# Order of the last filter inputs, the first queries and the keys' remainder in the head of a fused attention and spectral filter kernel

## The chip, the cores and the metric

The kernel runs on one core of a Trainium2 chip. What counts is the device time of one execution in microseconds, as the median over several executions. Two kernels that differ in the order of their work in the first 70 us are compared.

## What is computed

Two independent branches over S = 2048 positions and D = 448 channels are concatenated along the last axis:

```python
# A: attention, 16 query heads of 28 channels share one key and one value head
q = (x @ wq).reshape(B, S, 16, 28).transpose(0, 2, 1, 3)
k, v = x @ wk, x @ wv
p = softmax(einsum("bhqd,bkd->bhqk", q, k) * 28 ** -0.5)
a = einsum("bhqk,bkd->bhqd", p, v).transpose(0, 2, 1, 3).reshape(B, S, 448) @ wo
# B: a filter in the frequency domain
X = rfft2(x, axes=(-2, -1)) * (w_r + 1j * w_i)
b = irfft2(X, s=(S, D), axes=(-2, -1))
return concatenate([a, b], axis=-1)
```

All inputs are fp32. Products that need fp32 accuracy are made of two or three products of a rounded high part and a remainder (tiles ending in `h` and `l`).

## The kernel before

The kernel has a **head** (to about 68 us) and an **attention phase**. The attention phase runs 256 steps, each one group of four heads, one column of 512 queries and one block of 128 keys: four score matmuls (L917, 128x512, weights `ka`, moving `qa`), four exponentials on ACT (L852, or L928 and L942 for the scores set aside in tiles `k`), and four products with the values `vs` (L863). The later stages of the filter and the output projection are spread over these steps by a list (`PLAN`), and PE, ACT and DVE follow the order of the program.

The head does four things side by side:

- **Projection.** Twelve numbered groups (`group(n)`, preceded by a first column) multiply input and weights on PE (L369), and ACT evicts each result to `qraw` (L373); DVE takes each row's largest magnitude (L374), which `terms` turns into `prod` (L296) and `shift` into a bound `cvec` (a small matmul L301 and a DVE copy L302).
- **Keys.** `fetch` gathers half of the keys into `kf`. `keys(h)` for that half makes the high part on ACT (L287), the remainder `kl` on DVE (L288), and sends three copies (L293, on the sync queue) into `ka`: one of the high part, two of the remainder. Each half fills 64 columns of each of the 16 key blocks, so every score matmul reads both halves.
- **First queries.** `build_q(0, 0, True)` computes `ql` on DVE (L232), its high part `qh` on ACT (L229) and the remainder back into `ql` on DVE (L218). Sixteen copies (`copy_q(i, p, ...)`, head i, part p) then put them into `qa`: part 0 by DVE (L205), part 1 by ACT (L203), part 2 by the sync queue and part 3 by the GpSimd (POOL) queue (both L206).
- **Filter, first stages.** Eight inputs q = 0 to 7 of 512 KB (`xb`, L120) with a filter each (`fw`, L124). `fft1_fold(q)` is six DVE instructions (L129 to L134); `fft1_a(q)` 64 matmuls (L155) and two evictions on ACT into tiles `a` (L144); `fft1_b(q)` 16 matmuls (L172) into two PSUM tiles, evicted to `bs` by ACT for q < 6 (L180) and by DVE for q = 6, 7 (L182), and two stores of 225 KB to DRAM on the sync queue (L185). In a pair `fft1_b(q, q + 1)` the first takes two banks of their own, and the second takes two of the rotating banks.

PSUM has six rotating banks: `bank()` hands them out in turn. At the end of the head they are unpacked as `d, f, a, b, e, c = free` and put into the order in which attention takes them first. `a` was the bank of the last shift, `d` and `f` those of the last `fft1_a`, `b` that of the largest bound (`pb3`, read by L504), and `e` and `c` the two of `fft1_b(7)`.

PE's order is that of the program throughout, ACT's and DVE's from `group(4)` on (L451). The issue order on the sync and GpSimd queues is chosen when the program is built, after the order in the program and the time at which an instruction is thought to be ready. The attention phase starts when the last matmul of the head (L503) has been issued; `vs` comes from a transpose on DVE (L505) at the end of DVE's part of the head.

Of the kernel before, what the change touches and what calls it, by code (L numbers as in the profile page):

```python
# [10 lines left out]
F32 = mybir.dt.float32  # L11
# [4 lines left out]
ALU = mybir.AluOpType  # L16
# [6 lines left out]
DF = D // 2 + 1  # L23
# [49 lines left out]
def kernel(ctx: ExitStack, tc: tile.TileContext, t: dict):  # L73
    nc = tc.nc
# [4 lines left out]
    fp = ctx.enter_context(tc.tile_pool(name="fp", bufs=2))  # L79
# [8 lines left out]
    ka = cp.tile([128, S], F32R, name="ka")  # L88
# [4 lines left out]
    t1 = dp.tile([64, 64, DF], F32, name="t1")  # L93
# [10 lines left out]
    def aux2(name):  # L104
        return aux_pool[0].tile([128, 2, DF], F32, name=name, tag="aux")
# [9 lines left out]
    def fft1_load(q, parts=(0, 1)):  # L115
        if q > 7:
            return
        if 0 in parts:
            x = fp.tile([128, 4, 256], F32, name="xb", tag=("wr", "b2")[q % 2])
            nc.sync.dma_start(x, t["xb"][q])  # L120
            xb[q] = [x, None]
        if 1 in parts:
            w = xb[q][1] = fp.tile([128, 4, 64], F32, name="fw", tag=("ph", "pl")[q % 2])
            nc.sync.dma_start(w, t["fw"][:, 4 * q:4 * q + 4])  # L124

    def fft1_fold(q):
        x = xb[q][0][:113]
        f = fp.tile([113, 4, 256], F32, name="f", tag="wi")
        nc.vector.tensor_tensor(f[:, 0:2], x[:, 0::2], x[:, 1::2], op=ALU.add)  # L129
        nc.vector.tensor_tensor(f[:, 2:4], x[:, 0::2], x[:, 1::2], op=ALU.subtract)  # L130
        nc.vector.tensor_tensor(x[:, 0], f[:, 0], f[:, 1], op=ALU.add)
        nc.vector.tensor_tensor(x[:, 1], f[:, 0], f[:, 1], op=ALU.subtract)
        nc.vector.tensor_tensor(x[:, 2], f[:, 2], f[:, 3], op=ALU.subtract)
        nc.vector.tensor_tensor(x[:, 3], f[:, 2], f[:, 3], op=ALU.add)  # L134
        ff[q] = x.rearrange("p k (j h m) -> p k j h m", h=2, m=32)

    at1, stored = {}, []

    def fft1_a(*qs):
        for q in qs:  # L140
            for p in range(2):
                pa = fft1_a_mm(q, p)
                a = at1[q, p] = fp.tile([128, 2, DF], F32, name="a", tag=("pwr", "pwi")[p])
                nc.scalar.activation(a, pa, AF.Copy)  # L144
            fft1_load(q + 4, (0,))
# [10 lines left out]
                           start=True, stop=True)  # L156
        return pa

    def fft1_b(*qs):
        for i, q in enumerate(qs):  # L160
            fft1_out(q, fft1_mm(q, [pair_of(bank()) for _ in range(2)] if i else None))
            fft1_load(q + 4, (1,))

    def fft1_mm(q, pb=None):
        w = xb[q][1]
        if pb is None:
            pb = aux2("pbb"), ps_o.tile([128, 2, DF], F32, name="po")
        for p in range(2):
            a = at1.pop((q, p))
            for h in range(2):  # L170
                for e in range(2):
                    mm(pb[h][64 * e:64 * e + 64, p], w[64 * h:64 * h + 64, 2 * p + e], a[64 * h:64 * h + 64, e],  # L172
                       start=True, stop=True)
        return pb

    def fft1_out(q, pb):
        bs = fp.tile([128, 2, 2, DF], F32, name="bs", tag="cst" if q < 6 else "b2")
        for h in range(2):
            if q < 6:
                nc.scalar.activation(bs[:, h], pb[h], AF.Copy)  # L180
            else:
                nc.vector.tensor_copy(bs[:, h], pb[h])  # L182
        for e in range(2):
            n0 = 16 * e + 2 * q
            stored.append(nc.sync.dma_start(t1.rearrange("s (l n) f -> s l n f", l=2)[:, :, n0:n0 + 2],  # L185
                                            bs[64 * e:64 * e + 64]))

    def fft2_consts():
        for n in ("g1", "g2"):
# [9 lines left out]
    def copy_q(i, p, q, src, eng):  # L199

        o, x = q[32 * p:32 * p + 32, i], src[32 * i:32 * i + 32].bitcast(F32)
        if eng is nc.scalar:
            return eng.activation(o, x, AF.Copy)  # L203
        if eng is nc.vector:
            return eng.tensor_copy(o, x)  # L205
        return eng.dma_start(o.bitcast(F32), x)  # L206

    def build_q(c, g, first=False):
        cs = slice(c * CW, (c + 1) * CW)
        qh = qp.tile([128, CW], F32R, name="qh", bufs=1)  # L210
        ql = qp.tile([128, CW], F32R, name="ql", bufs=1)
        qt = ql.bitcast(F32)
        if (c, g) not in qa:
            qa[c, g] = qp.tile([128, 4, CW], F32R, name="qa")
        q = qa[c, g]

        def split():
            nc.vector.tensor_tensor(ql, qt, qh.bitcast(F32), op=ALU.subtract)  # L218
            if first:
                return  # L220
            for i in range(4):
                for p, src in enumerate((qh, ql)):
                    mv = nc.sync.dma_start(q[32 * p:32 * p + 32, i].bitcast(F32), src[32 * i:32 * i + 32].bitcast(F32))
                    behind(mv, b2["last", 0] if (c, g) == (0, 1) else stored[-1])
            nc.sync.dma_start(q[64:128].bitcast(F32), q[0:64].bitcast(F32))

        def high():
            if first:
                return nc.scalar.activation(qh, qt, AF.Copy)  # L229
            return nc.vector.tensor_copy(qh, qt)  # L230

        ops = [(540, lambda: nc.vector.tensor_scalar(qt, qraw[:, g, cs], mask, cvec[:, g, c:c + 1],  # L232
                                                     op0=ALU.mult, op1=ALU.add)),
               (450, high), (710, split)]
        if not first:
            return ops
        for _, op in ops:
            op()
        return q, qh, ql
# [9 lines left out]
    def bank():  # L249
        free.rotate(-1)  # L250
        return free[-1]

    def pair_of(b):
        return b[:, :2 * DF].rearrange("p (n f) -> p n f", n=2)


    with tc.tile_pool(name="w1", bufs=1) as w1:
# [24 lines left out]
        def keys(h):  # L282
            hs = slice(h * 1024, h * 1024 + 1024)
            kl = w1.tile([32, 1024], F32R, name="kl")
            src = kf[:, hs].rearrange("p (s t j) -> p s t j", s=2, j=32)
            high = ka[:32].rearrange("p (t s j) -> p s t j", s=NC, j=32)[:, 2 * h:2 * h + 2]
            nc.scalar.activation(high, src, AF.Copy)  # L287
            nc.vector.tensor_tensor(kl.rearrange("p (t s j) -> p s t j", s=2, j=32), src, high.bitcast(F32),  # L288
                                    op=ALU.subtract)
            kt = ka.rearrange("p (t x) -> p t x", t=16)[:, :, 64 * h:64 * h + 64]  # L290
            low = kl.rearrange("p (t x) -> p t x", t=16)
            for p, src in ((1, kt[:32]), (2, low), (3, low)):
                nc.sync.dma_start(kt[32 * p:32 * p + 32].bitcast(F32), src.bitcast(F32))  # L293

        def terms(c0, c1):
            return nc.vector.tensor_scalar(prod[:, :, c0:c1], qmx[:, :, c0:c1], kmb, None, op0=ALU.mult)  # L296
# [1 line left out]
        def shift(c0, c1):  # L298
            b = bank()[:, :NG * (c1 - c0)]
            pb = b.rearrange("p (g c) -> p g c", g=NG)  # L300
            mm(b, blk, prod[:, :, c0:c1], start=True, stop=True)  # L301
            nc.vector.tensor_copy(cvec[:, :, c0:c1], pb)  # L302

        halves = slice(0, 1024), slice(1024, 2048)
        with tc.tile_pool(name="x1", bufs=2) as x1:
# [125 lines left out]
            def group(n):  # L431
                c, g = 1 + n // 4, n % 4
                pq = pq1[g] if c == 1 else bank()
                for j in range(1 if c == 1 else 0, NK):
                    proj(pq, *xs[c], g, j)
                if n == 10:
                    key_max()
                evac(c, g, pq)
# [18 lines left out]
            for j in range(NK):  # L457
                split_x(*xs[3], 3, j)
            group(5)
            keys(0)  # L460
            group(6)
            fft1_fold(4)
            group(7)
            for v in range(3):
                fetch_v(range(7, 14), v)
            fft1_b(0, 1)
            fft1_a(2, 3)
            fft1_fold(5)
            group(8)
            group(9)  # L470
# [4 lines left out]
            terms(0, 1)  # L475
            fft1_fold(7)
            fetch_v(range(7, 12), 3)
            fft1_b(2, 3)
            keys(1)
            fft1_a(4, 5)  # L480
            shift(0, 1)
            qf, qh, ql = build_q(0, 0, True)
            group(11)
            terms(1, NC)


        for i in range(4):
            copy_q(i, 2, qf, qh, nc.sync)
            copy_q(i, 0, qf, qh, nc.vector)
            copy_q(i, 3, qf, ql, nc.gpsimd)  # L490
        fetch_v(range(12, 14), 3)
        copy_q(0, 1, qf, ql, nc.scalar)
        fft1_b(4, 5)
        copy_q(1, 1, qf, ql, nc.scalar)
        fft1_a(6, 7)
        for i in (2, 3):
            copy_q(i, 1, qf, ql, nc.scalar)
        shift(1, NC)
        nc.vector.tensor_reduce(cmax, cvec, axis=AX.X, op=ALU.max)
        pb3 = bank()  # L500
        fft1_b(6, 7)
        for g in range(NG):
            mm(pb3[0:1, 4 * g:4 * g + 4], cmax[:, g:g + 1], sel4, start=True, stop=True)  # L503
        nc.vector.tensor_reduce(bits, pb3[0:1, 0:16], axis=AX.X, op=ALU.max)  # L504
# [4 lines left out]

    d, f, a, b, e, c = free  # L510
    free.clear()
    free.extend((a, d, f, e, c, b))
    spare = a, b, d
    free = [[0.0, bank] for bank in free]
    clock = {"pe": 0.0, "act": 0.0, "dve": 0.0}
# [65 lines left out]
    b2 = {}  # L581
# [602 lines left out]
```

## Time and profile before

| | |
|---|---|
| three runs, us | 632.76, 632.44, 632.50 |
| median, us | 632.5 |
| profiled execution, us | 633.24 |
| its span (first to last instruction), us | 631.5 |
| granted TensorE clock, mean | 1.00 |

The rows of the profile that follow in the prediction have these columns. In a timeline: start in us from the span's beginning, duration, engine, line, operation, what is written and read, shape, number of merged instructions, and in brackets the idle time of the engine before it with what ended that. PEld is the loading of matmul weights, which overlaps the matmuls; SPq is an issue on the sync queue. Consecutive matmuls overlap, so a matmul's length says little, and the distance from start to start is its cost. In a table of windows: the stretch and its length, then for PE, PEld, DVE, ACT and POOL the busy time (number of instructions), then the clock, the mean busy share of the DMA engines and the GB/s moved. In a list of DMA issues the last number is the median time from issue to landing.

### The profile page before, as it was taken

The numbers are of one execution on the slowest core, as the hardware profiler recorded it, in microseconds if no ns is written. First come the engines' busy times: TensorE is split into PE (matmuls) and PEld (weight loads), VectorE is DVE, ScalarE is ACT, GpSimd is POOL, SyncE is SP. The second block draws the span as 40 slices with busy tenths as digits, with TensorE's granted clock in tenths as the row PEclk, the third lists the DMA queues.
The fourth block names the chain that finished last, engine by engine and source line by source line (L and its number), as shares of the span: only waits on it lengthen the run. The fifth ranks groups of instructions, "written<-read, shape, count | busy, mean of one in ns | idle before, by whom it ended". The sixth has DMA issues, their size and how long they took to land. (4 is left out here: it accounts for less than half of the span.)

```text
span 631.5 us, 12130 instructions
## 1 busy us (share of the span) xinstructions
PE 625.5 (99%) x4420; PEld 377.6 (60%) x4420; DVE 430.2 (68%) x775; ACT 547.2 (87%) x986; POOL 67.4 (11%) x132
## 2 busy tenths in 40 slices
PE   9999999999999999999999999999999999999997
PEld 7888545655555556646555665555556565555555
DVE  5996458779999944857766845277687764457753
ACT  5565999999999998988899989999989989989991
POOL 3522211011203110000110100001010100000000
PEclk9999999999999999999999999999999999999999
DMA  8857773446456523126340513034152413030001
GB/s 255 290 162 199 215 181 99 103 132 184 121 156 144 149 56 83 59 70 184 80 113 6 128 35 82 16 84 147 42 122 60 111 46 89 16 82 15 17 30 62
DMA packets 40931, 66.71 MB, mean 106 GB/s; under 512 B 11189, under 2 KB 25926, under 8 KB 39904
## 3 DMA queue, kind: packets, MB, share of 16 engines
q1 hardware_dynamic: 35232, 52.50, 30.4%
q0 software_dynamic: 5056, 12.45, 7.6%
q8 instruction: 36, 0.59, 0.4%
q10 hardware_dynamic: 576, 0.92, 0.4%
q14 instruction: 31, 0.25, 0.1%
HBM read 29.77 MB, written 17.87 MB: 75 GB/s over the span
## 5 line engine op out<-in xcount | busy, mean ns | idle before, releaser
L852 ACT ACTIVATE p<-s 128x512 f32<-128x512 f32 x392 | 217.8, 646 | 24.9 <-PE s L917 23.9
L917 PE MATMUL s<-qa,ka 128*128 128x512 f32 x736 | 222.6, 402 | 0.0
L917 PEld LDWEIGHTS s<-qa,ka 128*128 128x128 f32 x736 | 134.5, 188 | 58.6 <-issue 26.2
L863 PE MATMUL s<-p,vs 128*32 128x512 f32 x1144 | 141.7, 595 | 0.0
L923 DVE COPY k<-s 128x512 f32<-128x512 f32 x119 | 78.2, 685 | 68.1 <-PE s L917 67.9
L942 ACT ACTIVATE k<-k 128x1024 f32<-128x1024 f32 x80 | 83.4, 1140 | 0.0
L852 ACT ACTIVATE qraw<-s 128x512 f32<-128x512 f32 x136 | 78.0, 646 | 2.3 <-PE s L917 2.3
L863 PEld LDWEIGHTS s<-p,vs 128*32 128x32 f32 x1144 | 34.3, 109 | 76.2 <-issue 69.7
L852 ACT ACTIVATE p<-po 128x512 f32<-128x512 f32 x88 | 57.2, 650 | 6.5 <-PE po L917 6.4
L917 PE MATMUL po<-qa,ka 128*128 128x512 f32 x151 | 60.9, 404 | 0.0
L917 PE MATMUL sx<-qa,ka 128*128 128x512 f32 x137 | 55.2, 403 | 0.0
L863 PE MATMUL s<-qraw,vs 128*32 128x512 f32 x424 | 54.8, 593 | 0.0
L863 PE MATMUL s<-k,vs 128*32 128x512 f32 x352 | 46.3, 594 | 0.0
L852 ACT ACTIVATE p<-sx 128x512 f32<-128x512 f32 x64 | 42.0, 656 | 3.0 <-PE sx L917 2.9
L738 POOL DMA_DIRECT2D ol<-ol x36 | 18.0, 508 | 229.3 <-DVE ol L761 157.2
L867 DVE STREAM_TRANSPOSE osb<-s 128x512 f32<-128x512 f32 x15 | 10.7, 716 | 38.9 <-PE s L863 38.8
L917 PEld LDWEIGHTS po<-qa,ka 128*128 128x128 f32 x151 | 28.4, 188 | 13.6 <-issue 6.7
L917 PEld LDWEIGHTS sx<-qa,ka 128*128 128x128 f32 x137 | 25.7, 188 | 11.0 <-issue 4.2
L863 PEld LDWEIGHTS s<-qraw,vs 128*32 128x32 f32 x424 | 13.2, 110 | 29.9 <-issue 28.7
L863 PEld LDWEIGHTS s<-k,vs 128*32 128x32 f32 x352 | 11.0, 110 | 25.1 <-issue 24.2
L852 ACT ACTIVATE qraw<-sx 128x512 f32<-128x512 f32 x35 | 22.7, 648 | 2.0 <-PE sx L917 2.0
L923 DVE COPY p<-s 128x512 f32<-128x512 f32 x37 | 24.1, 682 | 0.0
(260 smaller groups left out, 926.2 us busy)
## 6 DMA issues: line engine op xcount, KB each, us to landing
qa<-qa SPq DMA_DIRECT2D x15, 512.0 KB
raw<-xa SPq DMA_DIRECT2D x16, 256.0 KB
xb<-xb SPq DMA_DIRECT2D x8, 512.0 KB
qa<-qh SPq DMA_DIRECT2D x64, 64.0 KB
qa<-ql SPq DMA_DIRECT2D x60, 64.0 KB
t<-bs SPq DMA_DIRECT2D x16, 225.0 KB
wr<-wr POOLq DMA_DIRECT2D x16, 225.0 KB, 3.9
wi<-wi POOLq DMA_DIRECT2D x16, 225.0 KB, 5.1
```

What stands on the lines that cost most here:

```text
L738: nc.gpsimd.dma_start(ol[c][o, g].bitcast(F32), ol[c][r, 0].bitcast(F32))
L852: nc.scalar.activation(tiles[-1][:, h % 2], sc, AF.Exp, scale=SCALE)
L863: mm(po[c, g][32 * i:32 * i + 32], vs[:, kc], ps[i // 2][:, i % 2], start=(n == 1), stop=(n == 16))
L867: nc.vector.transpose(o, po[c, g])
L917: begun.append(mm(sc, ka[:, kc * 128:(kc + 1) * 128], qa[c, g][:, h], start=True, stop=True))
L923: nc.vector.tensor_copy(keep[i][h // 2][:, h % 2], sc)
L942: nc.scalar.activation(p, p, AF.Exp, scale=SCALE)
```

## The change

Stores are taken out of `fft1_b` into a function `fft1_store(q)`, which also loads the filter q + 4. `fft1_b` handles one q; its second argument says whether it takes rotating banks. `keys` returns a function `finish` with the remainder and the three sends. The order in the head becomes: the loads of inputs 6 and 7 (issued by `fft1_a(2, 3)`) ahead of the stores of q = 1; the high part of the second half of the keys behind `fft1_a(4, 5)`; then shift and first queries, all sends of the queries, two DVE copies and one ACT copy; then the keys' remainder and its sends; then group 11. One copy (head 3, part 1) goes from ACT to DVE, one (head 2, part 1) from behind to ahead of the evictions of `fft1_a(6, 7)`, and the second eviction of `fft1_b(7)` from DVE to ACT. The order of the banks changes in its last three places. Nothing is added to or left out of the computation.

```diff
-    def fft1_b(*qs):
-        for i, q in enumerate(qs):
-            fft1_out(q, fft1_mm(q, [pair_of(bank()) for _ in range(2)] if i else None))
-            fft1_load(q + 4, (1,))
...
+    def fft1_b(q, other=False):
         w = xb[q][1]
+        pb = [pair_of(bank()) for _ in range(2)] if other else (aux2("pbb"), ps_o.tile([128, 2, DF], F32, name="po"))
...
+        bs = stored[q] = fp.tile([128, 2, 2, DF], F32, name="bs", tag="cst" if q < 6 else "b2")
         for h in range(2):
-            if q < 6:
+            if q < 6 or q + h == 8:
                 nc.scalar.activation(bs[:, h], pb[h], AF.Copy)
             else:
                 nc.vector.tensor_copy(bs[:, h], pb[h])
+
+    def fft1_store(q):
         for e in range(2):
             n0 = 16 * e + 2 * q
...
+            stored[-1] = nc.sync.dma_start(t1.rearrange("s (l n) f -> s l n f", l=2)[:, :, n0:n0 + 2],
+                                           stored[q][64 * e:64 * e + 64])
+        fft1_load(q + 4, (1,))
...
             nc.scalar.activation(high, src, AF.Copy)
...
+            def finish():
+                nc.vector.tensor_tensor(kl.rearrange("p (t s j) -> p s t j", s=2, j=32), src, high.bitcast(F32),
+                                        op=ALU.subtract)
...
+                for p, x in ((1, kt[:32]), (2, low), (3, low)):
+                    nc.sync.dma_start(kt[32 * p:32 * p + 32].bitcast(F32), x.bitcast(F32))
+            return finish
...
-            keys(0)
+            keys(0)()
...
-            fft1_b(0, 1)
+            fft1_b(0)
+            fft1_store(0)
+            fft1_b(1, True)
             fft1_a(2, 3)
+            fft1_store(1)
...
-            fft1_b(2, 3)
-            keys(1)
+            fft1_b(2)
+            fft1_store(2)
+            fft1_b(3, True)
+            fft1_store(3)
             fft1_a(4, 5)
+            finish_keys = keys(1)
             shift(0, 1)
             qf, qh, ql = build_q(0, 0, True)
+            for i in range(4):
+                copy_q(i, 2, qf, qh, nc.sync)
+                copy_q(i, 3, qf, ql, nc.gpsimd)
+            for i in (0, 1):
+                copy_q(i, 0, qf, qh, nc.vector)
+            copy_q(0, 1, qf, ql, nc.scalar)
+            finish_keys()
             group(11)
             terms(1, NC)
...
-        for i in range(4):
-            copy_q(i, 2, qf, qh, nc.sync)
+        for i in (2, 3):
             copy_q(i, 0, qf, qh, nc.vector)
-            copy_q(i, 3, qf, ql, nc.gpsimd)
         fetch_v(range(12, 14), 3)
-        copy_q(0, 1, qf, ql, nc.scalar)
-        fft1_b(4, 5)
         copy_q(1, 1, qf, ql, nc.scalar)
+        fft1_b(4)
+        fft1_store(4)
+        fft1_b(5, True)
+        fft1_store(5)
+        copy_q(2, 1, qf, ql, nc.scalar)
         fft1_a(6, 7)
-        for i in (2, 3):
-            copy_q(i, 1, qf, ql, nc.scalar)
+        copy_q(3, 1, qf, ql, nc.vector)
         shift(1, NC)
...
-        fft1_b(6, 7)
+        fft1_b(6)
+        fft1_store(6)
+        fft1_b(7, True)
+        fft1_store(7)
...
-    free.extend((a, d, f, e, c, b))
+    free.extend((a, d, f, c, b, e))
```

More of the change, by code (lines that the diff above doesn't have):

```diff
@@ L135, in fft1_fold @@
         ff[q] = x.rearrange("p k (j h m) -> p k j h m", h=2, m=32)
-    at1, stored = {}, []
+    at1, stored = {}, {}
     def fft1_a(*qs):
@@ L157, in fft1_a_mm @@
         return pa
-    def fft1_b(*qs):
-        for i, q in enumerate(qs):
-            fft1_out(q, fft1_mm(q, [pair_of(bank()) for _ in range(2)] if i else None))
-            fft1_load(q + 4, (1,))
-    def fft1_mm(q, pb=None):
+    def fft1_b(q, other=False):
         w = xb[q][1]
-        if pb is None:
-            pb = aux2("pbb"), ps_o.tile([128, 2, DF], F32, name="po")
+        pb = [pair_of(bank()) for _ in range(2)] if other else (aux2("pbb"), ps_o.tile([128, 2, DF], F32, name="po"))
         for p in range(2):
@@ L173, in fft1_mm @@
                        start=True, stop=True)
-        return pb
-    def fft1_out(q, pb):
-        bs = fp.tile([128, 2, 2, DF], F32, name="bs", tag="cst" if q < 6 else "b2")
+        bs = stored[q] = fp.tile([128, 2, 2, DF], F32, name="bs", tag="cst" if q < 6 else "b2")
         for h in range(2):
-            if q < 6:
+            if q < 6 or q + h == 8:
                 nc.scalar.activation(bs[:, h], pb[h], AF.Copy)
@@ L182, in fft1_out @@
                 nc.vector.tensor_copy(bs[:, h], pb[h])
+    def fft1_store(q):
         for e in range(2):
             n0 = 16 * e + 2 * q
-            stored.append(nc.sync.dma_start(t1.rearrange("s (l n) f -> s l n f", l=2)[:, :, n0:n0 + 2],
-                                            bs[64 * e:64 * e + 64]))
+            stored[-1] = nc.sync.dma_start(t1.rearrange("s (l n) f -> s l n f", l=2)[:, :, n0:n0 + 2],
+                                           stored[q][64 * e:64 * e + 64])
+        fft1_load(q + 4, (1,))
     def fft2_consts():
@@ L287, in keys @@
             nc.scalar.activation(high, src, AF.Copy)
[L288 to L293, printed above, removed]
+            def finish():
+                nc.vector.tensor_tensor(kl.rearrange("p (t s j) -> p s t j", s=2, j=32), src, high.bitcast(F32),
+                                        op=ALU.subtract)
+                kt = ka.rearrange("p (t x) -> p t x", t=16)[:, :, 64 * h:64 * h + 64]
+                low = kl.rearrange("p (t x) -> p t x", t=16)
+                for p, x in ((1, kt[:32]), (2, low), (3, low)):
+                    nc.sync.dma_start(kt[32 * p:32 * p + 32].bitcast(F32), x.bitcast(F32))
+            return finish
         def terms(c0, c1):
```

## The prediction

> **What bounds the kernel now.** I read the page first, then stretches of 10 us and of 1 us, then the timeline of each engine around the one stretch that was not full.
>
> ```profile
> span 631.5 us, 12130 instructions
> ...
> PE 625.5 (99%) x4420; PEld 377.6 (60%) x4420; DVE 430.2 (68%) x775; ACT 547.2 (87%) x986; POOL 67.4 (11%) x132
> ```
> ```profile
> 50.00:60.00 10.00, 10.00 (x187) 8.37 (x185) 7.95 (x18) 5.44 (x11) 2.48 (x5) 1.00 0.65 202
> ...
> 80.00:90.00 10.00, 9.91 (x51) 5.66 (x53) 3.95 (x7) 10.00 (x23) 1.92 (x4) 1.00 0.78 175
> ```
> ```profile
> 65.00:66.00 1.00, 0.50 (x10) 0.30 (x2) 0.34 (x2) 0.98 (x3) 1.00 (x2) 1.00 0.82 246
> ```
>
> The columns behind the stretch are its length and the busy time of PE, PEld, DVE, ACT and POOL, then clock, DMA share and GB/s. PE is the bound, at clock 1.00. The change touches only the head, and from 20 us on the head has one hole, at 65 to 72 us, where it hands over to attention. From 80 to 90 us, in early attention, ACT is as full as PE, so attention runs only as soon as both have started: what moves the first exponential moves everything behind it, up to the end. PE from the second hand-over of filter work to the third group of scores, weight loads where they say who was late:
>
> ```profile
> 60.19 0.41 PE L172 MATMUL pbb<-a,fw 64*64 64x225 f32 x2
> ...
> 61.87 3.30 PE L155 MATMUL s<-cs,xb 113*32 113x113 f32 x128
> 65.11 0.39 PE L301 MATMUL s<-prod,blk 128*128 128x12 f32 x2
> 66.04 0.41 PE L172 MATMUL pbb<-a,fw 64*64 64x225 f32 x2 [0.54 <-ACT a L144]
> ...
> 67.89 0.34 PE L503 MATMUL s<-sel,cmax 128*1 128x4 f32 x8
> 68.17 2.44 PE L917 MATMUL s<-qa,ka 128*128 128x512 f32 x8
> ...
> 71.85 0.50 PE L917 MATMUL s<-qa,ka 128*128 128x512 f32 x1
> ...
> 73.89 1.06 PE L863 MATMUL s<-k,vs 128*32 128x512 f32 x8
> 74.78 1.07 PE L863 MATMUL s<-p,vs 128*32 128x512 f32 x8
> 75.77 0.50 PE L917 MATMUL sx<-qa,ka 128*128 128x512 f32 x1
> ```
> ```profile
> 69.40 0.76 PEld L917 LDWEIGHTS s<-qa,ka 128*128 128x128 f32 x4 [0.33 <-DVE bs L182]
> ```
> ```profile
> 70.88 0.14 PEld L863 LDWEIGHTS s<-k,vs 128*32 128x32 f32 x2 [0.19 <-ACT k L928]
> ```
>
> From 65.11 to 71.85 PE takes 6.74 us for work that elsewhere takes 0.39 (shift) + 1.68 (a pair of second filter stages, 61.87 - 60.19) + 0.28 (68.17 - 67.89) + 2.04 (eight scores, 73.89 - 71.85) + 0.99 (one key block times values, 75.77 - 74.78) = 5.38. The hole is 1.36 us: 0.71 ahead of the first score, where PE waits for ACT's evictions `a`, and 0.65 behind it, where the fifth score waits for a bank that DVE empties and the fourth value product for ACT's fourth exponential. **1.36 us is the most that closing this hole can give.**
>
> **What sets the hole: ACT, and behind it DVE.**
>
> ```profile
> 55.68 1.06 ACT L287 ACTIVATE ka<-kf 32x1024 fp32r<-32x1024 f32 x1 [0.40 <-DMA kf<-qraw]
> 56.65 1.80 ACT L144 ACTIVATE a<-s 128x450 f32<-128x450 f32 x4
> 60.86 0.63 ACT L229 ACTIVATE qh<-ql 128x512 fp32r<-128x512 f32 x1 [2.41 <-DVE ql L232]
> 61.40 0.58 ACT L373 ACTIVATE qraw<-s 128x512 f32<-128x512 f32 x1
> 62.25 0.63 ACT L203 ACTIVATE qa<-ql 32x512 fp32r<-32x512 f32 x1 [0.28 <-DVE ql L218]
> 62.90 0.55 ACT L180 ACTIVATE bs<-pbb 128x450 f32<-128x450 f32 x1
> ...
> 63.77 0.99 ACT L180 ACTIVATE bs<-s 128x450 f32<-128x450 f32 x2
> ...
> 65.44 1.86 ACT L144 ACTIVATE a<-s 128x450 f32<-128x450 f32 x4
> 67.33 1.28 ACT L203 ACTIVATE qa<-ql 32x512 fp32r<-32x512 f32 x2
> 68.76 0.60 ACT L928 ACTIVATE k<-s 128x512 f32<-128x512 f32 x1
> ```
> ```profile
> 52.75 0.69 DVE L129 TENSOR_TENSOR f<-xb 113x512 f32<-113x512 f32 x1 [1.62 <-DMA xb<-xb]
> ...
> 58.96 1.21 DVE L288 TENSOR_TENSOR kl<-kf,ka 32x1024 fp32r<-32x1024 f32 x1
> ...
> 60.28 0.55 DVE L232 TENSOR_SCALAR ql<-qraw,mask,cvec 128x512 f32<-128x512 f32 x1
> 61.52 0.69 DVE L218 TENSOR_TENSOR ql<-ql,qh 128x512 fp32r<-128x512 f32 x1 [0.70 <-ACT qh L229]
> ...
> 62.99 1.76 DVE L205 CAST qa<-qh 32x512 fp32r<-32x512 f32 x4
> ```
>
> ACT idles 2.41 us for the first queries `ql`, which DVE makes late: it waited 1.62 us for input 6 (52.75), runs both folds to 58.96, and then does the keys' remainder `kl` (1.21) first. From 60.86 ACT is nearly full; its last `a` ends at 65.44 + 1.86 = 67.30, and the first score follows 0.87 later, at 68.17.
>
> **The change part by part.**
>
> Inputs 6 and 7 ahead of the stores. On the sync queue they move past two stores and a filter:
>
> ```profile
> 44.90 1.17 SPq L185 DMA_DIRECT2D t<-bs  x2
> 46.17 0.66 SPq L124 DMA_DIRECT2D fw<-fw  x1
> 46.93 0.56 SPq L120 DMA_DIRECT2D xb<-xb  x1
> ```
>
> They are issued 46.93 - 44.90 = 2.03 us earlier. Fold 6 can start once DVE is free, 52.75 - 1.62 = 51.13. Bounds: it gains 1.62 (it lands 2.03 earlier) or nothing (the transfer is paced by those ahead of it). I take 1.62, since two stores and a filter no longer go in front. Both folds then end at 58.96 - 1.62 = 57.34. The two stores and the filter come later; the first store is read only by the attention part's filter work, the filter by a stage at 60 us.
>
> Keys' high part behind the evictions, remainder behind the queries. PE's first filter stage ends here, with the shift matmul behind it:
>
> ```profile
> 55.79 1.54 PE L155 MATMUL s<-cs,xb 113*32 113x112 f32 x56
> ```
>
> ACT's last `a` of this pair can end at 57.33 + 0.07 + 0.55 = 57.95. The high part (1.06) runs to 59.01 and `qh` (0.63) to 59.66. `ql` is no limit: the shift ends at 57.33 + 0.39 = 57.72, and with some 0.2 for its copy and 0.55 for `ql` it is there at 58.5. So `qh` ends 61.49 - 59.66 = 1.83 earlier. Were inputs 6 and 7 no earlier, `ql` would be there at 58.96 + 0.2 + 0.55 = 59.7 at best and `qh` would end at 60.35, 1.14 earlier.
>
> ACT's chain afterwards. DVE's remainder of the queries (0.69) ends at 60.39. Then ACT: copy 60.42 to 61.05; eviction of group 11, overlapping it by 0.09, to 61.54; copy to 62.20; four `bs` (62.90 to 64.76, 1.86) to 64.08; the third copy, now in front, to 64.73; four `a` (1.86) to 66.61. The moves cost 0.66 for the third copy and 0.5 for the eviction, which is now queued behind the first copy and its 0.73 of waiting for DVE; who needs that eviction (the maximum for `prod`, the last value rows) has till 65.1 and beyond. The gain left is 67.30 - 66.61 = 0.69. The first score by this chain is at 66.61 + 0.87 = 67.48; PE alone could be there at 65.11 + 0.39 + 1.68 + 0.28 = 67.46, so ACT is hardly the limit any more.
>
> The fourth copy goes from ACT to DVE (some 0.44) and one `bs` of stage 7 from DVE to ACT. ACT is then idle from 66.61 until that `bs` at 67.3 and ends it by 67.9, ahead of the first exponential, which comes 68.76 - 68.17 = 0.59 behind the first score. Both cost nothing; without that cover the `bs` would cost 0.55. DVE needs the four casts at 0.44, the remainder 1.21 and 0.9 of small work between 60.39 and 65.1, when the shift needs `prod`: 1.0 us spare.
>
> Bank order. The fifth score finds its bank empty: 0.2 to 0.3 of waiting goes. But the fourth value product waits for the fourth exponential, 70.88 - 68.17 = 2.71 behind the first score, and that chain is unmoved by the fifth score. The gain is between 0 and 0.3; I take 0, since ACT ends last. In attention itself the order only renames banks.
>
> Sends. `qh` leaves at 59.7 instead of 61.60; the keys' transfers now come behind on the same queue.
>
> ```profile
> 60.20 1.31 SPq L293 DMA_DIRECT2D ka<-kl  x2
> 61.60 2.50 SPq L206 DMA_DIRECT2D qa<-qh  x4
> ```
> ```profile
> wi<-wi POOLq DMA_DIRECT2D x2, 225.0 KB, 5.8
> ...
> qa<-ql POOLq DMA_DIRECT2D x4, 64.0 KB, 3.2
> ```
>
> Four `qh` sends take 2.50, to 62.2; the key part that waits for nothing follows to 62.9. DVE has `kl` ready at 60.39 + 2 x 0.44 + 1.21 = 62.48, so its two sends are issued at 62.9 and 63.55 (0.65 each). When they land no row shows; these two views of 55 to 70 us bound it, 3.2 us for 64 KB and 5.8 for 225 KB. `kl` has 128 KB a send; on the straight line between them that is 4.2, which I take: 67.75. Every tile of keys holds a part of this transfer, so the first score needs all of it, and starts at 67.8 instead of 67.48. The bounds: landing 66.75 (no wait) and 69.35. The `ql` sends on POOL start 2 us earlier and land earlier.
>
> **The sum.** First score 67.8 against 68.17: 0.37 us less, carried to the end with the exponentials. Against the profiled execution (span 631.5, time 633.24, so 1.74 around it) the span becomes 631.1. That execution is 0.74 above the median of the runs, 632.5; taken off the median, **632.1 us**.
>
> **The rivals.**
>
> *The keys land late.* The wait moves from ACT's evictions to the second `kl` transfer. It decides once this lands later than 68.1, 4.6 us behind its issue, and then each microsecond late is one microsecond of the kernel. For it: POOL's loads of 225 KB move up together with the queries and then share the DMA engines, whose share is 0.82 in the quoted stretch. At 5.8 us the first score is at 69.4, 1.2 later: 633.7; with another 0.4 of contention 634.1. Against: four sends of 64 KB are now done before, and the keys need no more than an ordinary row here takes.
>
> [...]
>
> *Inputs 6 and 7 come no earlier.* Then `qh` gains 1.14 and not 1.83, ACT's last `a` ends at 67.3 and the engines start attention as before; the keys, issued at 64.2, land at 68.4, 0.3 late: 632.8. For it: fold 6 waits for a landing that the transfers ahead may pace. Against: exactly those go behind.
>
> *The whole hole closes.* Keys in time, and the exponentials no longer hold the value products: 1.36 less, 631.1. For it: PE is then the only limit, and 67.46 is in reach. Against: the 2.71 us from first score to fourth product is ACT's own work, which nothing shortens.
>
> **How the numbers follow.** Forecast (631.6 to 632.4) 0.42; keys late 0.24; inputs no earlier 0.15; hole closed 0.19. A measurement of this kernel can tell about 0.2%, 1.26 us, from no change: the bounds are 631.24 and 633.76. Faster by more needs nearly the whole hole: 0.19. Slower by more needs the keys over 5.8 us: 0.16 of their 0.24, and 0.02 of the inputs' case: 0.18. The rest, 0.63, is within. The range reaches from the closed hole, 631.1, to the keys at 5.8 us, 633.7.
>
> **What would show it.** Fold 6 starting near 51.1 with no wait; `qh` ending near 59.7; the last `a` near 66.6; `kl` issued near 63; the first score between 67.5 and 67.8, and whether its wait names ACT or a DMA; no wait for DVE at the fifth score; the fourth product still 2.7 behind the first score. It is wrong if the first score comes later than 68.2, if PE gets a new wait before 65 us, or if the stretch from first score to end changes length by more than 0.3 us.

## The result, and the profile after

| | before | after |
|---|---|---|
| time, us, median (range) | 632.47 (631.87 to 634.23) | 637.57 (636.83 to 639.38) |
| ratio, 95% interval | | 1.0081 (1.0064 to 1.0099) |
| profiled execution: time, span, us | 633.24, 631.5 | 638.24, 636.5 |

The change makes the kernel 5.1 us slower, 0.8%; the forecast was 632.1, the range ended at 633.7. First the page of the kernel after: PE has nearly the same busy time (625.4 beside 625.5) in a span that is 5.0 us longer.

```profile
span 636.5 us, 12129 instructions
...
PE 625.4 (98%) x4420; PEld 378.7 (60%) x4420; DVE 430.2 (68%) x775; ACT 547.6 (86%) x986; POOL 67.0 (11%) x132
```

The timelines of ACT, DVE and the sync queue of after, in the stretch that the prediction followed. Line numbers are those of the new file: `ql` is made at L226, `qh` L223, `kl` L284 with its sends at L289, `a` still L144.

```profile
50.12 0.68 DVE L129 TENSOR_TENSOR f<-xb 113x512 f32<-113x512 f32 x1
...
60.02 1.21 DVE L284 TENSOR_TENSOR kl<-kf,ka 32x1024 fp32r<-32x1024 f32 x1
```
```profile
57.90 0.61 ACT L223 ACTIVATE qh<-ql 128x512 fp32r<-128x512 f32 x1
...
63.74 1.86 ACT L144 ACTIVATE a<-s 128x450 f32<-128x450 f32 x4
```
```profile
58.54 2.46 SPq L200 DMA_DIRECT2D qa<-qh  x4
61.04 0.64 SPq L289 DMA_DIRECT2D ka<-ka  x1
61.78 2.22 SPq L289 DMA_DIRECT2D ka<-kl  x2
64.10 3.91 SPq L178 DMA_DIRECT2D t<-bs  x4
```

Fold 6 no longer waits, `qh` ends at 58.51, the last `a` at 65.60, and the keys' remainder is on its way at 61.78, each 1.0 to 1.2 us ahead of the forecast. (Some 0.9 us of that is not the change's: the first projection matmul starts at 4.61 us in both executions, but the seventh at 6.29 here and at 7.21 before, in a part that the change does not touch.) Now PE, from the shift matmul on:

```profile
64.17 0.39 PE L298 MATMUL s<-prod,blk 128*128 128x12 f32 x2
...
66.19 0.34 PE L516 MATMUL s<-sel,cmax 128*1 128x4 f32 x8
71.60 3.75 PE L930 MATMUL s<-qa,ka 128*128 128x512 f32 x8 [5.06 <-DMA t<-bs]
75.28 1.18 PE L876 MATMUL s<-k,vs 128*32 128x512 f32 x8
76.39 0.50 PE L930 MATMUL s<-qa,ka 128*128 128x512 f32 x1
```

PE was ready for the first score at 66.5, as the ACT chain had promised, and then waited **5.06 us for a DMA**. The releaser printed, a store `t<-bs`, is not what the score reads; it takes its turn later on the semaphore that the second send of `kl` uses. What the score reads is `ka`, and the last piece of `ka` is that send, issued at 62.43. The trace has sixteen updates of the semaphore for it, between 67.21 and 71.46 us (fourteen of them by 69.67): the last, which is taken as the landing, is 9.03 us behind the issue and 0.14 ahead of the first score. POOL's timeline, and after it the DMA windows of 62 to 64 and 65 to 67 us, show what stands beside it:

```profile
62.64 1.07 POOL L606 DMA_DIRECT2D wr<-wr  x2
63.70 1.04 POOL L606 DMA_DIRECT2D wi<-wi  x2
```
```profile
DMA packets 1017, 0.38 MB, mean 189 GB/s; under 512 B 964, under 2 KB 964, under 8 KB 1016
```
```profile
DMA packets 408, 0.44 MB, mean 222 GB/s; under 512 B 358, under 2 KB 358, under 8 KB 408
## 3 DMA queue, kind: packets, MB, share of 16 engines
q0 software_dynamic: 72, 0.36, 78.1%
q1 hardware_dynamic: 336, 0.08, 22.6%
```

Of the packets under 512 B, 853 of the 964 and 331 of the 358 are the 256 B packets of the keys; the rest are records of 4 B. Until POOL's loads start to move, 964 of them pass in 2 us; afterwards 358, and POOL's queue (q0), with 50 packets of 7200 B, holds 78% of the engines' time. By the trace's packet records the three sends of the keys are 1536 packets of 256 B, of which the last ends at 70.63, and the 128 packets of `wr` and `wi` start between 64.07 and 70.00. The 900 KB of `wr` and `wi` are the first filter loads of the attention phase. In the first profile of before they were issued at 65.49, 4.6 us behind the second send of `kl`; now 0.2 us behind it, because the `ql` sends that precede them on POOL's queue moved up.

There is a second cost. These are 1 us windows of after (length; busy time of PE, PEld, DVE, ACT, POOL; clock; DMA share; GB/s):

```profile
67.00:68.00 1.00, 0.00 (x0) 0.00 (x0) 1.00 (x4) 0.00 (x0) 0.00 (x0) 1.00 0.94 216
68.00:69.00 1.00, 0.00 (x0) 0.00 (x0) 0.93 (x3) 0.00 (x0) 0.00 (x0) 0.87 1.02 252
69.00:70.00 1.00, 0.00 (x0) 0.00 (x0) 0.52 (x1) 0.00 (x0) 0.00 (x0) 0.50 1.02 350
...
74.00:75.00 1.00, 1.00 (x4) 0.54 (x2) 0.00 (x0) 1.00 (x4) 0.00 (x0) 0.50 0.31 96
75.00:76.00 1.00, 1.00 (x9) 0.20 (x8) 0.00 (x0) 1.00 (x4) 0.00 (x0) 0.72 0.06 22
```

While PE idles its granted clock falls to 0.50, at 68.74, and stays there until 75.56, so the first eight scores and value products run at half the clock: 71.60 to 76.39 is 4.79 us, against 3.69 before (68.17 to 71.85).

**The account of the two profiled executions**, in stretches of PE's own time (the shift is counted from its second matmul, 0.13 behind the row's start): start to shift 64.31 against 65.24; shift to first score 7.29 against 2.93; first to ninth score 4.79 against 3.69; ninth score to the end 560.09 against 559.63. That is -0.93, +4.36, +1.10 and +0.46, together +5.0.

### The profile page after: what moved, and what is told of

Same layout as the page of the kernel before. It is cut to its first block, busy times and chain, and to the rows that moved or that the text cites. A ratio compares the mean times of both kernels' runs of the same rounds, so it can differ in the third digit from the quotient of the medians.

```text
span 636.5 us, 12129 instructions
## 1 busy us (share of the span) xinstructions
PE 625.4 (98%) x4420; PEld 378.7 (60%) x4420; DVE 430.2 (68%) x775; ACT 547.6 (86%) x986; POOL 67.0 (11%) x132
## 5 line engine op out<-in xcount | busy, mean ns | idle before, releaser
L930 PEld LDWEIGHTS s<-qa,ka 128*128 128x128 f32 x736 | 136.0, 190 | 63.6 <-issue 31.2
```

The source lines that it names most:

```text
L930: begun.append(mm(sc, ka[:, kc * 128:(kc + 1) * 128], qa[c, g][:, h], start=True, stop=True))
```

## The experiments

Two theories of the wait. **Contention** (A in the expectations): the keys' send is slow since POOL's loads run beside it. **The send itself** (B): its 256 B runs, or its place behind the query sends, make it slow. All kernels in one table, times as median of runs, the ratio against runs of the kernel before that were timed beside it, stretches in us from the profiled executions (several where a kernel was profiled again):

| kernel | time | ratio to before | shift to 1st score | 1st to 9th score | 9th score to end |
|---|---|---|---|---|---|
| before | 632.47 | | 2.93; 2.14; 2.14 | 3.69; 3.69; 3.68 | 559.6; 560.2; 559.7 |
| after | 637.57 | 1.0081 (1.0064 to 1.0099) | 7.29; 5.98 | 4.79; 4.53 | 560.1; 560.3 |
| after, POOL's loads held | 632.63; 632.20 | 1.0003 (0.9993 to 1.0013); 0.9999 (0.9990 to 1.0008) | 2.17; 2.16 | 3.69; 3.68 | 560.3; 560.3 |
| after, only `wi` held | 636.51 | 1.0060 (1.0042 to 1.0077) | 5.24 | 4.57 | 560.1 |
| after, keys ahead of queries | 635.33 | 1.0048 (1.0031 to 1.0065) | 4.67 | 3.97 | 559.4 |
| before, keys behind queries | 639.01 | 1.0110 (1.0092 to 1.0128) | 6.86 | 4.35 | 559.5 |
| before, POOL's loads held | 632.45 | 1.0011 (0.9999 to 1.0023) | 2.14 | 3.68 | 559.7 |
| after, PE kept busy, 21 matmuls | 638.73 | 1.0099 (1.0078 to 1.0119) | 7.74 | 3.66 | 561.3 |
| after, PE kept busy, 17 matmuls | 637.81 | 1.0083 (1.0066 to 1.0100) | 6.85 | 3.66 | 561.2 |
| after, `wr`, `wi` in shorter pieces | 637.63 | 1.0070 (1.0042 to 1.0097) | 5.64 | 5.55 | 560.3 |

**POOL's loads held.** In the changed kernel `wr` and `wi` of the first fold pair wait for the last score issued.

```diff
-                behind(ld, begun[-1], q == 1)
+                behind(ld, begun[-1], q <= 1)
```

> The changed kernel, with one wait more: the four filter loads on the GpSimd queue (wr and wi of q = 0, 225 KB each) are issued only once PE has begun the scores of the second step. Theory A (those loads, running on the same DMA engines, hold up the keys' second remainder transfer): the transfer lands 3 to 4 us after its issue instead of 9, the first score no longer waits for it and follows the last head matmul by some 0.3 us, at 66.5 to 67.5; the time falls by some 5 to 6 us to 631.3 to 632.3. Theory B (the transfer is late because it stands behind the query transfers on the sync queue and consists of small packets): nothing changes, the first score stays near 71.6 and the time at 637.5.

The whole loss is gone: 632.63 beside 632.41 of before. The DMA window of 63 to 65 us and PE's timeline, from the same kernel run and profiled again:

```profile
DMA packets 1436, 0.37 MB, mean 187 GB/s; under 512 B 1427, under 2 KB 1427, under 8 KB 1435
```
```profile
66.28 0.34 PE L516 MATMUL s<-sel,cmax 128*1 128x4 f32 x8
66.55 2.23 PE L930 MATMUL s<-qa,ka 128*128 128x512 f32 x8
```

1427 small packets pass in these 2 us, 890 in the same stretch of after. The first score starts 0.27 behind the matmuls ahead of it, with no wait. The sends of `kl` leave at the same place (61.92 and 62.58). Counted from the first of them, 1678 packets under 512 B pass in 4 us here and 1189 in after, which needs 7 us for 1691. The last key packet ends at 66.01 and the second send has landed at 66.33, 3.75 us behind its issue (3.70 in the other profile of this kernel) instead of 9.03. That refutes "the send itself": the same 256 B runs, in the same place behind the query sends, land in 3.75 us with POOL's loads held. But the kernel is not faster than before either (the 631.3 to 632.3 that were expected are missed by 0.3), though its first score is 0.76 nearer to the shift than in the first profile of before. That is taken up below.

**Only `wi` held.** Half of POOL's bytes are left beside the keys.

```diff
-                behind(ld, begun[-1], q == 1)
+                behind(ld, begun[-1], q == 1 or q == 0 and n == "wi")
```

> As the first run, but only the two wi loads wait; the two wr loads (450 KB) stay early. Theory A: about half of the hold-up, the second remainder transfer lands at 67 to 69 and the first score begins then; time 633 to 635. Theory B: 637.5 as the changed kernel. If it is the presence and not the amount of large packets that counts, nearly all of the hold-up stays until 450 KB are through, 68 to 69.

```profile
70.61 3.08 PE L930 MATMUL s<-qa,ka 128*128 128x512 f32 x8 [3.02 <-DMA t<-bs]
```

A wait of 3.02 us is left of 5.06 (3.75 in a second profile of after), and 4.1 of the 5.1 us of loss; the expected 633 to 635 was missed. The cost goes with POOL's bytes, but not in proportion: `wr` comes first, and the second send, issued at 63.49, still takes 6.98 us to land, against 9.03 (7.71 in the second profile) and 3.75. From 65 to 67 us 574 small packets pass, against 358 in after, where the sends left 1.05 us earlier:

```profile
DMA packets 616, 0.43 MB, mean 213 GB/s; under 512 B 574, under 2 KB 574, under 8 KB 616
```

**Keys ahead of queries.** Everything of the change, but the remainder and its sends directly behind the high part.

```diff
-            finish_keys = keys(1)
+            keys(1)()
...
-            finish_keys()
```

> The changed kernel, with only the place of the keys' remainder undone: subtraction and the three transfers come directly behind the high part, ahead of the shift and the first queries. Everything else of the change stays, the early filter loads too. Theory A: the transfers are over by 62 to 63, before the filter loads reach the DMA engines at 64; no wait of the first score for a DMA; the queries come 1.0 to 1.2 us later, so the first score is at 67 to 68 and the time 632 to 632.8. Theory B expects the same here, so this run only tells whether the place of the remainder is the cause at all. If another part of the change were the cause (bank order, evictions, input loads), the time would stay above 636.

The expectation was missed by 2.5 us. No DMA wait, as expected (the sends are issued at 59.54), but the high part stands behind ACT's evictions in the changed order, DVE waits for it and makes the queries late. DVE, ACT, then PE of this kernel:

```profile
58.30 1.21 DVE L284 TENSOR_TENSOR kl<-kf,ka 32x1024 fp32r<-32x1024 f32 x1 [1.62 <-ACT ka L281]
```
```profile
60.21 0.63 ACT L223 ACTIVATE qh<-ql 128x512 fp32r<-128x512 f32 x1 [1.94 <-DVE ql L226]
```
```profile
65.00 0.39 PE L298 MATMUL s<-prod,blk 128*128 128x12 f32 x2 [0.48 <-ACT bs L171]
66.66 0.41 PE L166 MATMUL pbb<-a,fw 64*64 64x225 f32 x2 [1.27 <-ACT a L144]
...
69.81 2.52 PE L929 MATMUL s<-qa,ka 128*128 128x512 f32 x8
```
```profile
64.00:65.00 1.00, 0.52 (x24) 0.28 (x12) 0.97 (x3) 1.00 (x4) 1.00 (x3) 1.00 0.61 193
65.00:66.00 1.00, 0.39 (x2) 0.30 (x2) 0.56 (x3) 0.98 (x2) 1.00 (x2) 1.00 0.40 99
66.00:67.00 1.00, 0.34 (x8) 0.21 (x8) 0.00 (x0) 0.98 (x4) 1.00 (x3) 1.00 0.67 88
67.00:68.00 1.00, 1.00 (x20) 0.65 (x16) 0.00 (x0) 0.92 (x3) 0.05 (x1) 0.59 0.85 333
68.00:69.00 1.00, 1.00 (x17) 0.66 (x12) 0.88 (x2) 0.00 (x0) 0.00 (x0) 0.50 1.18 285
```

`qh` ends 2.3 us later than in after, PE waits 0.48 and 1.27, and its clock halves soon after 67, during the last filter stages. So the queries' place ahead of the remainder does carry weight once the high part has moved behind the evictions; one half of the move without the other is no improvement.

**Keys behind queries, alone.** The kernel before, with only the remainder and its three sends moved behind the queries' copies.

```diff
-            keys(1)
+            finish_keys = keys(1)
...
             copy_q(i, 3, qf, ql, nc.gpsimd)
+        finish_keys()
```

> The kernel before, with only the keys' remainder and its three transfers moved, to behind the query copies; nothing else of the change. If this move alone is the cause: the second remainder transfer is issued near 65.5, beside the filter loads, lands 6 to 9 us later, at 71.5 to 74.5; the first score waits for it; the time is 636 to 641. If it needs the rest of the change, the time is below 634.

```profile
64.64 1.29 SPq L295 DMA_DIRECT2D ka<-kl  x2
```
```profile
64.10 1.04 POOL L597 DMA_DIRECT2D wr<-wr  x2
65.15 1.03 POOL L597 DMA_DIRECT2D wi<-wi  x2
```
```profile
71.91 3.42 PE L921 MATMUL s<-qa,ka 128*128 128x512 f32 x8 [4.65 <-DMA wi<-wi]
```

639.01, at least as much as the whole change costs (the profiled execution, 637.53, is the fastest of four). The second send of `kl`, which PE waits for, is issued at about 65.3, behind `wr` and beside `wi`. This one move is enough for the loss.

**Does the hold cost what the head gains?** The hold removed the wait and with it the hole of 0.71 us of which the prediction spoke, and yet the kernel was no faster than before. The same edit to the kernel before:

```diff
-                behind(ld, begun[-1], q == 1)
+                behind(ld, begun[-1], q <= 1)
```

> The kernel before with one edit: POOL's loads wr and wi of the first fold pair wait for the last score issued, as those of the second do already. In the changed kernel the same edit gave 632.63 with a first score 0.76 us nearer to the shift matmul, and yet no shorter time than before. Theory C (the edit itself costs later, since the first outputs of the second transform come later): the kernel before with it is 0.5 to 0.9 slower, 632.9 to 633.3. Rival (it costs nothing; the 0.76 is absorbed by a bound behind it that does not depend on when scores start): 632.2 to 632.7.

> The changed kernel with POOL's loads wr and wi held, once more beside the kernel before with the same edit, to compare the two at a few tenths. If the head's gain of 0.76 us reaches the end once both carry the same edit, it is 0.5 to 0.9 below the kernel before with the hold; if it is absorbed behind the head, the two differ by less than 0.3.

632.45 and 632.20, beside 632.23: no cost of the hold that could be told, and no gain of the changed order that could be told either. (The runs of the kernel before with the hold spread from 631.52 to 634.32. By medians the two kernels differ by 0.25, by means by 0.6, so the times alone do not exclude a gain of 0.5 to 0.9; the stretches, 2.14 and 2.16, show none at the first score.) But the kernel before with the hold also has its first score 2.14 behind the shift, not 2.93, though nothing ahead of 65 us was edited. So the 2.93 itself came into question.

**The kernel before, profiled again.**

> The kernel before as it is, profiled a second time. The prediction read a wait of 0.71 us ahead of the first score (2.93 us from the shift matmul to the first score, where the work alone is 2.2) out of one execution, which was 0.74 slower than the median. With POOL's loads held and nothing else edited, which cannot reach back to instructions before 65 us, the same stretch was 2.14. Theory D (that wait belongs to the one profiled execution, where input 6 landed late, not to the kernel): 2.1 to 2.3 us here, qh ending 5.1 to 5.2 ahead of the shift matmul instead of 3.8. Rival (the wait belongs to the kernel and holding the loads removed it): 2.8 to 3.0.

> The kernel before as it is, a third time, for the same question: Theory D 2.1 to 2.3 us from the shift matmul to the first score, or now and then 2.9; the rival 2.8 to 3.0 each time.

DVE and PE of the third profile:

```profile
50.77 0.69 DVE L129 TENSOR_TENSOR f<-xb 113x512 f32<-113x512 f32 x1 [0.31 <-DMA xb<-xb]
```
```profile
64.43 0.39 PE L301 MATMUL s<-prod,blk 128*128 128x12 f32 x2
...
66.43 0.34 PE L503 MATMUL s<-sel,cmax 128*1 128x4 f32 x8
66.70 2.54 PE L917 MATMUL s<-qa,ka 128*128 128x512 f32 x8
```

Input 6 is 0.31 late here, 0.70 in the second profile, 1.62 in the first; only the 1.62 reaches the first score. In both others the first score stands 0.27 behind the matmuls ahead of it: **the hole of 0.71 us was of one execution in three, not of the kernel.** How often it comes no run tells. These two executions took 632.93 and 631.86, so the hole is not all that makes one execution slower than another.

**The kernel after, profiled again.**

> The changed kernel as it is, profiled a second time: if the keys' landing is set by what runs beside it and not by the one execution, the first score again comes 7.0 to 7.6 us behind the shift matmul, and the eight scores take 4.6 to 4.9 with the clock at 0.50 for some 6 us. If it varies as the kernel before does, 6.0 to 7.0.

```profile
70.83 3.49 PE L930 MATMUL s<-qa,ka 128*128 128x512 f32 x8 [3.75 <-DMA t<-bs]
```

The wait is there again, at 3.75 instead of 5.06, and the first score 5.98 behind the shift, just less than either case of the expectation. The second send lands 7.71 us behind its issue here. The wait varies by more than a microsecond, and the loss with it (636.83 to 639.38 in the runs of this kernel, 637.46 in this execution).

**PE kept busy in the wait.** 21, then 17 matmuls whose result is not read, behind the last matmul of the head.

```diff
         nc.vector.transpose(vs.rearrange("p t d -> p (t d)"), vt)
+        for _ in range(21):
+            mm(pb3[:, 256:384], ident, ident, start=True, stop=True)
```

> The changed kernel with 21 more f32 matmuls (identity by identity, 128x128, into unused columns of pb3's bank) on PE behind the eight of pb3 and ahead of the first score; their result is not read. They leave the wait for the keys as it is and only keep PE busy in it. Theory A (the loss has two parts: 5.06 us of waiting for the keys' second send, of which the clock that halves after it, 0.50 from 69 to 75 us, makes a further 1.10): the first score still starts 5.4 us behind pb3's matmuls, near 71.6, the granted clock stays at 1.00, the eight scores and what is between them take 3.69 us again and not 4.79, time 1.1 below the changed kernel, 636.0 to 637.0. Rival (the slower scores come from what else runs beside them, the clock has no price): clock or not, 4.8 us again and 637.0 to 638.0. Rival (the matmuls do not fit in the wait): the first score starts later than 72.0 and the time is not below 637.5.

> The changed kernel with 17 instead of 21 identity matmuls ahead of the first score, so that they end before the keys land (21 ended 0.45 us behind the point at which the first score started without them). Clock theory: first score 7.2 to 7.5 behind the shift matmul, the eight scores 3.7, the ninth score 11.0 behind the shift matmul instead of 12.1; total 636.4 to 637.2 if this reaches the end. If attention takes the gain back, as it did with 21 (556.7 us from the ninth score to the last matmul instead of 555.8): 637.3 to 638.3.

PE and one window of the kernel with 17 (each of these fp32 matmuls is two records):

```profile
67.34 4.06 PE L520 MATMUL s<-ident 128*128 128x128 f32 x34 [0.81 <-DVE bits L517]
71.16 2.20 PE L932 MATMUL s<-qa,ka 128*128 128x512 f32 x8
...
74.82 0.51 PE L932 MATMUL s<-qa,ka 128*128 128x512 f32 x1
```
```profile
72.00:73.00 1.00, 1.00 (x6) 0.64 (x4) 0.00 (x0) 1.00 (x3) 0.00 (x0) 1.00 1.02 308
```

The clock stays at 1.00 and first to ninth score takes 3.66 in both: the 0.9 to 1.1 us in that stretch are the clock's. The gain in the total did not come: neither kernel is faster than after. With 21 it is the rival in which the matmuls do not fit into the wait, with 17 the case in which the gain is taken back (637.3 to 638.3). There are two reasons. The matmuls outlast the keys: the second send has landed at 71.03 with 21 and at 69.81 with 17, but the first score follows the matmuls at 72.01 and 71.16, so they take back 1.0 and 1.35 us themselves. From the shift to the ninth score the two kernels need 11.40 and 10.51 us, after in its two profiles 12.08 and 10.51. And ninth score to end became 561.3 and 561.2 instead of 560.1 and 560.3. One place of that is an output projection in mid attention, which waits for a transfer `oh<-ol`. Here after, then the kernel with 17:

```profile
370.24 0.44 PE L787 MATMUL s<-woh,oh 128*128 128x448 f32 x1 [0.46 <-DMA oh<-ol]
```
```profile
369.92 0.44 PE L789 MATMUL s<-woh,oh 128*128 128x448 f32 x1 [1.07 <-DMA oh<-ol]
```

PE got there earlier and waited 0.61 more. With 21 matmuls the same wait is only 0.7, so this place does not account for it there, and where the rest went is open. So the half clock is shown as a price of the eight scores; that the kernel's time would be lower by as much without it is not.

**Shorter pieces.** The tiles `wr` and `wi` are padded, so that rows no longer join in memory: does the length of POOL's pieces set how late the keys land?

```diff
-            b2[n, q] = fp.tile([128, 4, DF], F32, name=n)
+            b2[n, q] = fp.tile([128, 4, DF + 8], F32, name=n)[:, :, :DF]
```

> The changed kernel with the tiles wr and wi padded by 8 numbers a row (225 to 233) and the filter work reading the first 225 of them: POOL's loads move the same bytes at the same place and time, but a row no longer joins its neighbour in memory, so that they should go in pieces of 900 B instead of 7200 B. [...] If the pieces stay at 7200 B in the trace, nothing is told.

Inconclusive: by the packet records POOL's pieces shrank from 7200 to 4500 and 900 B only. First score 5.64 behind the shift (5.98 and 7.29 in after), the second send 7.38 us from issue to landing (7.71 and 9.03), time 637.63. What the length of the pieces does beside their bytes is not shown. The clock was halved from 69.3 to 76.1 here, so first to ninth score took 5.55 (4.79 and 4.53 in after).

## Why the prediction was wrong

*Inputs 6 and 7 earlier, fold 6 without a wait.* Right: fold 6 at 50.12 directly behind the reduction ahead of it (with a wait of 0.22 in the second profile of after). But the 1.62 us gained were read from one execution; the kernel before loses 0.70 and 0.31 there in its other two.

*ACT's chain and the 0.69 us.* Right as arithmetic against the profiled execution: with the loads held, the first score came 0.76 nearer to the shift. As a gain of the kernel it was nothing, since before has the same 2.14 in its other two profiles. **The step "That execution is 0.74 above the median of the runs, 632.5; taken off the median" failed**: the slow execution held the very hole (2.93 - 2.14 = 0.79) that the sum then closed, so the sum took off once as an accident what it took off again as a gain. In the other two executions there is nothing to gain ahead of the first score.

*Evictions and bank order, 0.* Borne out: first to ninth score is 3.68 to 3.69 in before and in after with the loads held.

*The keys' landing.* **"on the straight line between them that is 4.2, which I take: 67.75" is the step that failed where the loss arose.** Without POOL's loads beside it the transfer is no slower than that: 3.70 and 3.75 us in the kernel with the loads held. In the changed kernel the second send, issued at 62.43, landed at 71.46, 9.03 us later (7.71 in the second profile), and held the first score until 71.60. The line was drawn between transfers by size, and did not ask what runs beside them, although the working itself moves POOL's `ql` sends up by 2 us and with them the 900 KB behind them on that queue.

*The rival "keys land late"* named the mechanism and its place, with 5.8 us of landing and 0.4 of contention for a worst of 634.1. The contention measured is 9.03 - 3.75 = 5.3 us in one execution and 7.71 - 3.75 = 4.0 in the other. The rival's worst, 634.1, fell short by 3.5.

*The clock.* No term of the sum held it; a wait was priced at its length ("each microsecond late is one microsecond of the kernel"). With waits of 5.06 and 3.75 us in the two profiles of after, the scores behind cost 1.10 and 0.85 more than the 3.69 and 3.68 of before. The clock is at a half for 6.8 us in the first profile of after and for 3.4 in the second. One long idle stretch was not needed: with the keys ahead of the queries it fell although no idle stretch was longer than 1.27 us and PE was busy for a third to a half of each of the three microseconds ahead of it. Half clock lasted 3.41 us there. Over as long a stretch that ends at the fall PE was busy for 0.49 there (to 67.17) and for 0.36 in the first profile of after (to 68.74); with PE kept busy, no such stretch had less than 0.76, and the clock stayed. What makes it fall is not shown beyond that.

*The stretch behind* changed by 0.46 between the two profiles, over the 0.3 that the prediction named, but before alone spreads over 559.6 to 560.2, so this sign tells nothing.

## What to carry to other kernels

When a producer moves up on one queue, list everything queued behind it there: those transfers move up too (here `wr`, from 4.6 to 0.2 us behind the keys' second send), and their bytes meet whatever is still in flight on the other queues. A transfer on the critical path is to be priced by what runs beside it (here 9.03 and 7.71 us beside POOL's loads, 3.75 and 3.70 without them), and large loads that nobody needs soon are best tied to an event behind it (632.63 and 632.20 with the hold, 637.57 without). And before a hole is counted as gain, look whether it is in more than one execution (the 0.71 us here were in one of three): a profile that is slower than the median may show the accident rather than the kernel.

## What the hardware showed unasked

- Beside 50 packets of 7200 B of POOL's queue in 2 us (78% of the engines' time), the packets under 512 B fell to 358, from 964 in the 2 us window before POOL's loads moved.
- The sixteen completions of one 128 KB send spread over 4.25 us in after (67.21 to 71.46), and the last two came 1.6 us behind the fourteenth. With the loads held they spread over 1.24 and 0.26 us in two executions.
- The same kernel's wait for the same transfer was 5.06 and 3.75 us in two executions.
- The total did not follow the head one to one: with PE kept busy the stretch behind the ninth score grew by 0.9 to 1.2 us, with 17 matmuls 0.61 of it in a wait for one transfer 300 us later.
